# Five kinds of copies dealt out anew and one list of tasks replaced by a longer one, in a fused attention and two-layer feed-forward kernel

## The chip, the cores and the metric

The kernel runs on 1 core of a Trainium2 chip. The metric is device microseconds of one execution. Three runs of the kernel before took 588.29 to 589.33 us, median 588.75 us.

## The reference

Attention of 2 batches, 8 heads, 576 positions and 64 dimensions, with a bias on the scores that a small network makes from the two positions. Its output, 1152 tokens of 512, goes through two feed-forward layers of 512 by 2048 by 512, all in float32:

```python
scores = scale * np.matmul(q, k.transpose(0, 1, 3, 2))
x = (np.log1p(np.abs(rel)) / psi_i)[..., None]     # rel = i - j; psi_i depends on i
bias = np.maximum(x @ w1 + b1, 0.0) @ w2            # 32 hidden, 8 heads
scores = scores + bias.transpose(2, 0, 1)[None]
attn = np.exp(scores - np.max(scores, axis=-1, keepdims=True))
attn = attn / (np.sum(attn, axis=-1, keepdims=True) + 1e-09)
x = np.matmul(attn, v)                              # then to (B*S, H*D)
h = x @ w_in0                                       # first layer
g = s * np.maximum(h, 0.0) ** 2 + b
x = g @ w_out0
h = x @ w_in1                                       # second layer
out = (h * np.tanh(np.log1p(np.exp(h)))) @ w_out1
```

## The kernel before

*Attention.* The work is cut into units: a pair of heads hp, a tile t of 128 queries (the fifth tile has 64), a batch b. The two batches of one (hp, t) make a duo; `ORDER` gives the 20 duos. For a (hp, b) the loads of q and k (`Pair.load`, L486 and L490, SyncE) land in two staging buffers `raw`; a copy packs them into `nat` (`Pair.pack`, L499: for six of the eight pairs, the first two are loaded into `nat` directly); TensorE transposes `nat` to `t` (`Pair.turn`, L527); two copies (`put`, L301 on ScalarE or L303 on VectorE) take `t` out of PSUM into `qk`. For each unit TensorE makes the scores `s` (L571) in PSUM. VectorE adds the bias `nb` and takes the row minimum `mn` of the negated scores (`bias_and_max`, L581), ScalarE the exponential `e` (L591), GpSimd and VectorE the inverse sum and the division (L598, L602, L608). TensorE transposes `e` into `pp` (L622), a copy (`keep`) takes it out as `pt`, and TensorE multiplies with v (`values`, L642). What is left over of a duo's columns goes through `turn_rest` (L663) and `keep_rest`.

*The bias.* It depends on the difference of two positions and on the row, so it is made once, for 36 groups of 16 rows: rectified rows `r` (`bias_row`, L402 on VectorE, L399 on ScalarE), a product on TensorE in two pieces (`bias_products`, L412), copies out as `bo` (`bias_out`, L305 on VectorE, L301 on ScalarE), a mirrored part (`bias_mirror`, L434, on ScalarE or GpSimd), a store to DRAM (`bias_store`, L438). A load `nb` (`load_bias`, L454) reads back the rows of a tile for a pair of heads; it waits for the stores of those rows. The fifth tile, with 64 rows, is the first in `ORDER`.

*The feed-forward layers.* Every float32 product is three products of rounded parts. A weight tile `raw` (512 KB: `rawi` of the first matrix, `rawo` of the second; i0 to i15 and o0 to o15) is loaded (L272, into one of two staging buffers), widened on ScalarE in two steps (L278, L279), joined on VectorE (L284), and split into its rounded part `whi` (`high`, L303) and the difference `wli` (`low`, L297). The tokens stand in three blocks j of 384. A block's hidden group (L1032, 12 matmuls) makes `h` of block j and tile f; relu, a square and two halves follow (L1042, L1045, L1086); the sums (L1109) collect `y`. Hidden groups are named h0_0_4 for layer 0, block 0, tile 4. Eight weight tiles, `WEARLY`, are loaded and converted while the attention still runs; for the others buffers come free when it ends.

*What sets the order.* Nothing is left to a scheduler at run time: each engine works through its own list. `Plan` makes the lists. Every step is a `Task` with an engine, a price in us, what it comes after and the buffers that it takes (`Hold`, numbers in `BUFS`). `WHO` says, a letter for each task, which engine does a copy that two engines could do (v VectorE, a ScalarE, p GpSimd). `SEQ` gives a place in one common row to every task that it names; `Plan.run` takes these in that row, each started as early as its engine and its predecessors allow by the planner's own prices. A task without a place is put in by its start and its rank, once no task of the row that is still due takes the same kind of buffer. Only the order goes into the program; the prices don't.

Of the kernel before, what the change touches and what calls it, by code (L numbers as in the profile page):

```python
# [21 lines left out]
def attention_bias_then_two_moe(ctx: ExitStack, tc: tile.TileContext, ins, out):  # L22
# [24 lines left out]
        'bias_row': 'vvaavavvvvvvvaaaavvvavaavavvvvaavavaavaavavavavvavavavvvvvavvavavavavavvvavvvaavvavvaaavavvvvvvavvaaavaavavavvavvaaaaavvvavvavvaavaavavvvvaaavva',  # L47
        'bias_out': 'avaavvavaaaaavavaaavvaavvaaaaaaavavvavavvaaa',
        'bias_mirror': 'ppapapppppappaaapppppappapppppppapaa',
        'pack': 'vpvpvv',  # L50
        'put': 'vvvaavaaavvvaavavava',
        'keep': 'aaaavvvvaavavvavvvavvaaaavaaaaaavaavavav',
        'keep_rest': 'aaaavvaaaaavavvvvvaa',
# [6 lines left out]
            7, 14, 1, 6, 85, 89, 97, 102, 137, 148, 163, 166, 56, 59, 241, 244,  # L60
        ),
        'bias_row': (
# [5 lines left out]
        ),  # L68
        'bias_products': (
            11, 13, 18, 21, 28, 30, 35, 37, 57, 60, 67, 71, 83, 86, 118, 132, 90, 112, 155, 162, 209, 183, 231, 228, 247, 275, 320, 291, 348, 316,  # L70
            368, 373, 421, 467, 418, 465, 509, 511, 544, 549, 571, 599, 626, 624,
        ),
        'scale_lx': (
            15,
        ),
        'bias_out': (
            16, 17, 24, 26, 33, 34, 39, 43, 62, 63, 77, 84, 87, 98, 133, 139, 114, 125, 164, 174, 217, 195, 245, 233, 260, 295, 343, 298, 357, 333,
            375, 388, 440, 481, 422, 474, 514, 536, 551, 559, 590, 608, 634, 628,
        ),
        'bias_mirror': (  # L80
            47, 29, 36, 45, 69, 116, 120, 182, 145, 160, 177, 180, 222, 200, 258, 254, 271, 344, 351, 353, 389, 400, 446, 454, 472, 493, 489, 479,
            523, 548, 572, 568, 593, 621, 638, 633,
        ),
        'bias_store': (
            54, 40, 38, 48, 82, 121, 124, 191, 149, 169, 181, 192, 253, 249, 293, 261, 296, 346, 360, 356, 427, 403, 452, 458, 475, 503, 494, 499,
            557, 556, 576, 605, 600, 630, 642, 635,
        ),
        'Pair.turn': (
            53, 44, 126, 151, 197, 223, 95, 299,
        ),  # L90
        'Pair.put': (
            61, 58, 68, 80, 50, 134, 140, 158, 161, 159, 207, 211, 232, 230, 229, 100, 99, 306, 308, 309,
        ),
        'Unit.scores': (
            73, 104, 143, 168, 216, 236, 265, 285, 307, 325, 359, 378, 402, 425, 455, 477, 497, 518, 553, 589, 611, 632, 649, 669, 685, 702, 724, 742,
            765, 781, 802, 819, 838, 853, 873, 888, 904, 921, 939, 952,
        ),
        'load_bias': (
# [600 lines left out]
    class Plan:  # L699
# [51 lines left out]
        def run(self):  # L751
# [18 lines left out]
            while given or any(left.values()):  # L770
# [521 lines left out]
```

## Time and profile before

| | |
|---|---|
| median of three runs | 588.75 us |
| the profiled execution | 587.15 us |
| its span | 585.4 us |
| TensorE busy | 570.3 us |
| VectorE busy | 461.5 us |
| ScalarE busy | 374.9 us |
| GpSimd busy | 100.9 us |

The span goes from the first to the last instruction of the program; the profiled execution's own time has a little more around it. A busy time is the sum over an engine's instructions, with nothing of how they stand to each other. The attention fills about the first 180 us, the two feed-forward layers the rest. In the rows below PE is TensorE, PEld its weight load, DVE VectorE, ACT ScalarE, POOL GpSimd, and SP SyncE, from whose queue nearly all DMAs are issued.

### The profile page before, as it was taken

Reading aid. Unit: us, or ns where it says so; the run is one execution under the profiler, and the core shown is the slowest. Engines: PE = TensorE matmul, PEld = TensorE weight load, DVE = VectorE, ACT = ScalarE, POOL = GpSimd, SP = SyncE. Lnnn points to the kernel's source line nnn. Section 1 sums busy time; section 2 is a strip of 40 time slices with the busy share of each in tenths; the row PEclk is TensorE's granted clock in tenths of the full one; section 3 lists DMA queues with packets and bytes.
Section 4 is the critical chain, followed back from the end, with each engine's and each line's share of the span. In section 5 each row is a group of like instructions: output and inputs, shape, how many; then the busy total and the mean of one; then the engine's idle time right before and its main releaser. Section 6 shows DMA issues by size and latency. Waiting matters only on the chain. (4 is left out here: it accounts for less than half of the span.)

```text
span 585.4 us, 12492 instructions
## 1 busy us (share of the span) xinstructions
PE 570.3 (97%) x4740; PEld 509.6 (87%) x4740; DVE 461.5 (79%) x1001; ACT 374.9 (64%) x761; POOL 100.9 (17%) x255
## 2 busy tenths in 40 slices
PE   8699999999999999999999999999999999999997
PEld 5356777888889999999999999989999899999895
DVE  5789899899856999433236999999998788898795
ACT  6799899999965687442224678666554445454453
POOL 2353656567650000000000000000000000000000
PEclk9899999999999999999999999999999999999999
DMA  6899667786404668400000667500000100010001
GB/s 158 239 297 261 209 200 246 238 249 213 146 3 126 234 221 277 151 1 1 1 0 1 209 218 257 180 0 2 0 2 0 55 1 0 1 54 1 1 1 54
DMA packets 50375, 65.99 MB, mean 113 GB/s; under 512 B 17548, under 2 KB 34060, under 8 KB 50316
## 3 DMA queue, kind: packets, MB, share of 16 engines
q1 hardware_dynamic: 50040, 65.11, 35.4%
q8 instruction: 37, 0.61, 0.4%
q14 instruction: 22, 0.18, 0.1%
q10 hardware_dynamic: 276, 0.09, 0.1%
HBM read 51.94 MB, written 13.25 MB: 111 GB/s over the span
## 5 line engine op out<-in xcount | busy, mean ns | idle before, releaser
L608 POOL TENSOR_SCALAR e<-e,rs 128x576 f32<-128x576 f32 (+2 forms) x104 | 66.4, 653 | 17.4 <-DVE rs L602 14.7
L1032 PE MATMUL h<-xh,whi 128*128 128x384 f32 x192 | 64.8, 337 | 0.0
L1032 PE MATMUL h<-yh,wli 128*128 128x384 f32 x192 | 64.7, 337 | 0.0
L1032 PE MATMUL h<-yl,whi 128*128 128x384 f32 x192 | 64.6, 337 | 0.0
L1032 PE MATMUL h<-yh,whi 128*128 128x384 f32 x192 | 64.6, 336 | 0.0
L1032 PE MATMUL h<-xh,wli 128*128 128x384 f32 x192 | 64.4, 335 | 0.0
L1032 PE MATMUL h<-xl,whi 128*128 128x384 f32 x192 | 64.4, 335 | 0.0
L1045 DVE SCALAR_TENSOR_TENSOR u<-h,u 128x384 f32<-128x384 f32 x48 | 26.6, 554 | 42.2 <-ACT u L1042 42.2
L581 DVE CUSTOM_DVE_ANT_0 s<-s,nb 128x576 f32<-128x576 f32 x72 | 52.4, 751 | 6.4 <-PE s L571 5.2
L591 ACT ACTIVATE e<-s,mn 128x576 f32<-128x576 f32 x72 | 55.1, 768 | 3.3 <-DVE mn L581 2.7
L1061 ACT ACTIVATE r<-n,two 128x384 f32<-128x384 f32 x48 | 29.6, 616 | 42.0 <-DVE n L1057 42.0
L571 PE MATMUL s<-qk 64*128 64x144 f32 (+1 forms) x640 | 50.4, 297 | 2.7 <-ACT qk L301 1.5
L571 PEld LDWEIGHTS s<-qk 64*128 64x128 f32 (+1 forms) x640 | 41.7, 178 | 12.0 <-ACT qk L301 3.3
L1042 ACT ACTIVATE u<-h 128x384 f32<-128x384 f32 x48 | 23.2, 483 | 43.5 <-PE h L1032 43.5
L1053 ACT ACTIVATE u<-u 128x384 f32<-128x384 f32 x48 | 25.0, 520 | 33.1 <-DVE u L1050 33.1
L1109 PE MATMUL y<-gl,who 128*128 128x384 f32 (+1 forms) x192 | 44.6, 339 | 0.0
L1109 PE MATMUL y<-gh,wlo 128*128 128x384 f32 (+1 forms) x192 | 44.3, 337 | 0.0
L1109 PE MATMUL y<-gh,who 128*128 128x384 f32 (+1 forms) x192 | 44.3, 337 | 0.0
L1109 PE MATMUL y<-who,gh 128*128 128x512 f32 x144 | 43.3, 395 | 0.8 <-ACT y L1121 0.8
L1109 PE MATMUL y<-wlo,gh 128*128 128x512 f32 x144 | 43.3, 395 | 0.0
L1109 PE MATMUL y<-who,gl 128*128 128x512 f32 x144 | 43.2, 395 | 0.0
L399 ACT ACTIVATE r<-lx,bl 128x368 f32<-128x368 f32 (+17 forms) x63 | 38.6, 651 | 2.2 <-DVE bl L367 2.1
(99 smaller groups left out, 1354.2 us busy)
## 6 DMA issues: line engine op xcount, KB each, us to landing
rawi<-in_moe_w_in_dram SPq DMA_DIRECT2D x32, 512.0 KB, 3.8
rawo<-in_moe_w_out_dram SPq DMA_DIRECT2D x32, 512.0 KB, 4.5
nbias_d<-bo SPq DMA_DIRECT2D x36, 295.5 KB, 2.7
nb<-nbias_d SPq DMA_DIRECT2D x32, 288.0 KB, 4.5
natv<-in_v_dram SPq DMA_DIRECT2D x16, 128.0 KB, 5.5
out_dram<-ob SPq DMA_DIRECT2D x8, 256.0 KB, 2.5
raw<-in_q_dram SPq DMA_DIRECT2D x6, 288.0 KB, 5.9
raw<-in_k_dram SPq DMA_DIRECT2D x6, 288.0 KB, 4.9
```

The lines of the kernel that those rows point to most:

```text
L399: nc.scalar.activation(out=r, in_=src, func=AF.Relu, bias=bl[:, g : g + 1])
L571: nc.tensor.matmul(self.ps[rows, x if self.both else 2 * j + x, o : o + PIECE], st.qk[d, 0, self.q0 : self.q0 + self.w], st.qk[d, 1, c0 : ...
L581: nc.vector.tensor_tensor_reduce(out=self.s[n][:m], in0=self.ps[:m, 2 * n : 2 * n + 2, :HALF], in1=nb[:m].rearrange("p (n j) -> p n j", n= ...
L591: nc.scalar.activation(out=self.e[:m, (S + REST) * n :][:, :S], in_=self.s[n][:m].rearrange("p n j -> p (n j)"), func=AF.Exp, bias=self.mn ...
L608: nc.gpsimd.tensor_scalar(self.e[:m, y : y + w], self.e[:m, x : x + w], self.rs[:m, n : n + 1], 0.0, op0=ALU.mult, op1=ALU.add)
L1032: nc.tensor.matmul(self.ph, w[:, c * P : (c + 1) * P], x[:, c, :], start=(c == 0 and n == 0), stop=(c == KD - 1 and n == 2),)
L1042: nc.scalar.activation(out=self.u, in_=self.ph, func=AF.Relu)
L1045: nc.vector.scalar_tensor_tensor(self.u, self.ph, 0.0, self.u, op0=ALU.max, op1=ALU.mult)
L1053: nc.scalar.activation(out=self.z, in_=self.z, func=AF.Exp)
L1061: nc.scalar.activation(out=self.r, in_=self.n, func=AF.Ln, bias=two)
L1109: nc.tensor.matmul(o, a, c, start=(f == 0 and i == 0), stop=(f == NF - 1 and i == 2))
```

## The change

The instructions are the same; their order and, for the copies, their engines are others. Three things change. `WHO` deals the copies out anew: among others the first six `pack` copies go from `vpvpvv` to `avvapp` (in the planner's count, not in the order of time), and the four mirrors first in the count go to ScalarE. `SEQ` is another row: it had 1010 places, which ended with the first 16 hidden groups and held 8 weight tiles; it now has 1298, and holds 20 weight loads of the first matrices, 12 of the second (`load`), 32 conversions, and the blocks of the first layer up to sums of the second block. Last, the planner's prices of transfers (`us` the issue, `mb` the size) are changed, and its rule for tasks that have no place in the row: such a task now waits until no task of the row is left for its *engine*, where before it looked at kinds of buffers.

```diff
...
-        'bias_mirror': 'ppapapppppappaaapppppappapppppppapaa',
-        'pack': 'vpvpvv',
...
+        'bias_mirror': 'aaaapapappppppppaapapappppaapppaapap',
+        'pack': 'avvapp',
...
     SEQ = {
...
         'Pair.load': (
-            7, 14, 1, 6, 85, 89, 97, 102, 137, 148, 163, 166, 56, 59, 241, 244,
+            3, 8, 2, 14, 58, 74, 101, 103, 120, 123, 154, 165, 1, 57, 253, 262,
...
@@ -757,11 +791,11 @@
             pipe, port, form = PIPE, 0.0, 0
             self.made = []
 
-            due = [h.what for t in given for h in t.takes]
+            due = [t.engine for t in given]
 
             def key(t):
                 at = self.ready(t)
-                if at is None or t.seq is None and any(h.what in due for h in t.takes):
+                if at is None or t.seq is None and t.engine in due:
                     return None
                 dry = DRY if t.engine == "PE" and t.form != form else 0.0
                 start = max(at, free[t.engine], port if t.port else 0.0)
@@ -793,8 +827,7 @@
                     left[t.engine].remove(t)
                 else:
                     given.pop()
-                    for h in t.takes:
-                        due.remove(h.what)
+                    due.remove(t.engine)
                 for h in t.takes:
                     self.holds[h.what].append(h)
                 self.made.append(t)
@@ -824,7 +857,7 @@
 
     firstnb = [add("none", 0.0, 3, lambda: None)]
     stores, rowed = {}, []
-    lx0 = add("SP", 0.45, -150, load_lx, mb=0.3)
+    lx0 = add("SP", 0.45, -150, load_lx, mb=0.27)
     lx0 = add("POOL", 0.8, -150, scale_lx, after=[lx0])
 
     def clear_all():
@@ -858,7 +891,7 @@
             h1.users.append(o)
             outs.append(o)
         m = add_any({"a": ("ACT", 0.0008 * (BW - w) + 0.1), "p": ("POOL", 0.0012 * (BW - w) + 0.15)}, at + GRANK + 2, bias_mirror, G, after=outs)
-        stores[G] = add("SP", 0.5, at - 50, bias_store, G, after=[m], mb=0.3)
+        stores[G] = add("SP", 0.42, at - 50, bias_store, G, after=[m], mb=0.22)
         hb.users.append(stores[G])
 
 
@@ -870,7 +903,7 @@
         hr, hn, hold, hl = Hold("raw"), Hold("nat"), Hold(big), Hold("one")
         cut = n < CUT
         loads = [
-            fetch(1.35 if cut else 0.65, key, LLEAD, 0.6 if cut else 0.3, st.load, nm, cut, takes=[hn if cut else hr] if nm == "q" else [])
+            fetch(1.35 if cut else 0.65, key, LLEAD, 0.42 if cut else 0.28, st.load, nm, cut, takes=[hn if cut else hr] if nm == "q" else [])
             for nm in "qk"
         ]
         loads[1].behind = loads[:1]
@@ -898,7 +931,7 @@
                 h = Hold("nb")
                 after = [stores[G] for G in range(u.q0 // (RI * RI), (u.q0 + u.w) // (RI * RI))]
                 nbh[u.hp, u.t, n] = h, add("SP", 1.2 if u.both else 0.58, at - (80 if i > 1 else 400), load_bias, u.hp, u.t, u.heads(n), after=after,
-                                           takes=[h], mb=0.29)
+                                           takes=[h], mb=0.27)
                 nbh[u.hp, u.t, n][1].soft = [*issued[-1:], *([scored[i - NLEAD]] if i >= NLEAD else [])]
                 issued.append(nbh[u.hp, u.t, n][1])
                 firstnb[0].past = issued[:1]
@@ -919,7 +952,7 @@
             exps.append(x)
             if n == 0 and firsts[u.hp, u.b] == i:
                 hl = Hold("lastv")
-                lv = add("SP", 1.9, 10 * i + VRANK, stacks[u.hp, u.b].load_v, takes=[hl], mb=0.4)
+                lv = add("SP", 1.85, 10 * i + VRANK, stacks[u.hp, u.b].load_v, takes=[hl], mb=0.37)
                 lv.soft = [load, s]
                 valued[u.hp, u.b] = add("POOL", 0.55, 10 * i, stacks[u.hp, u.b].spread_v, after=[lv, zeros])
                 hl.users.append(valued[u.hp, u.b])
@@ -1002,7 +1035,7 @@
             load = w.load
         hr, hf, hw = Hold("wraw" + two), Hold("wf" + two), Hold(f"w{'a' if f < EARLY else 'b'}{nm}")
         new = [] if early else [opened]
-        t = add("SP", 0.42, at - 20, load, after=[ended, *(new if two else [])], takes=[hr], mb=0.52)
+        t = add("SP", 0.42, at - 20, load, after=[ended, *(new if two else [])], takes=[hr], mb=0.45)
         t = add("ACT", 1.12, at, w.widen, after=[t], takes=[hf])
         t = add("DVE", 0.6, at + 1, w.join, after=[t])
         hr.users.append(t)
```

Three places in the lists, a row an instruction: the line, the operation, what it writes and reads. The last number of a name counts buffers; what stands ahead of it tells the tile: of a unit batch, pair of heads, tile of queries (s_1_0_4: batch 1, heads 0, tile 4), of a pair batch and heads (t_0_3, t_3 for short), of a bias product its group and first column (bias_4_0), of a weight layer and tile (rawi_0_3 is i3 of layer 0). The lines of the changed kernel are 34 higher.

TensorE, in the first 30 us, where the pair `t_0_3` is transposed ahead of the second unit's scores `s_1_0_4`, before:

```order
L412 MATMUL bias_2_272_415<-r_11_349,w2b_123 32x272
L412 MATMUL bias_4_0_425<-r_16_365,w2b_123 32x512
L412 MATMUL bias_4_0_425<-r_17_358,w2b_123 32x512
L412 MATMUL bias_4_0_425<-r_18_376,w2b_123 32x512
L412 MATMUL bias_4_0_425<-r_19_385,w2b_123 32x512
L527 MATMUL t_0_3_441<-ident_66,nat_0_3_422 128x64 x18
L571 MATMUL s_1_0_4_473<-qk_1_0_273 64x144 x8
```

and now:

```order
L446 MATMUL bias_2_272_417<-r_11_381,w2b_123 32x272
L561 MATMUL t_0_3_433<-ident_66,nat_0_3_431 128x64 x18
L446 MATMUL bias_4_0_461<-r_16_425,w2b_123 32x512
L446 MATMUL bias_4_0_461<-r_17_400,w2b_123 32x512
L446 MATMUL bias_4_0_461<-r_18_427,w2b_123 32x512
L446 MATMUL bias_4_0_461<-r_19_405,w2b_123 32x512
L605 MATMUL s_1_0_4_479<-qk_1_0_302 64x144 x8
```

The four products of bias group 4 stood ahead of `t_0_3` and now stand behind it, ahead of the scores.

VectorE at the same place (`nat_0_3` is the packed pair, `mn_0_0_4_0` the minimum of the first unit), before:

```order
L402 TENSOR_SCALAR r_10_381<-lx0_113,bl_124 128x544
L402 TENSOR_SCALAR r_8_387<-lx0_113,bl_124 128x544
L303 COPY nat_0_3_422<-raw_0_3_327 128x1152
L581 ISA s_0_0_4_0_436,mn_0_0_4_0_437<-s_0_0_4_367,nb_0_4_0_378 128x576
L581 ISA mn_0_0_4_0_437 128x1
L305 TENSOR_SCALAR bo_2_420<-bias_2_272_415,li_115 128x272
L303 COPY qk_0_3_442<-t_0_3_441 128x576
```

and now:

```order
L436 TENSOR_SCALAR r_10_403<-lx0_113,bl_124 128x544
L436 TENSOR_SCALAR r_19_405<-lx0_113,bl_124 128x512
L337 COPY qk_1_0_302<-t_1_0_301 128x64x8
L615 ISA s_0_0_4_0_422,mn_0_0_4_0_423<-s_0_0_4_385,nb_0_4_0_371 128x576
L615 ISA mn_0_0_4_0_423 128x1
L339 TENSOR_SCALAR bo_2_453<-bias_2_0_411,li_115 128x272
L436 TENSOR_SCALAR r_23_455<-lx0_113,bl_124 128x496
L339 TENSOR_SCALAR bo_2_453<-bias_2_272_417,li_115 128x272
L337 COPY qk_0_3_434<-t_0_3_433 128x576
```

The copy `nat_0_3` is gone from VectorE ahead of the minimum (it is on GpSimd now); in its place stands a copy `qk_1_0`, and copies of bias sums have moved up.

SyncE's queue near the end of the attention (the rows nb are loads of bias rows: heads, tile, first head), before:

```order
L272 DMA rawi_0_3_2612<-in_moe_w_in_dram 128x4x256
L454 DMA nb_3_2_1_2634<-nbias_d_76 128x1x576
L272 DMA rawo_0_2_2736<-in_moe_w_out_dram 128x1024
L454 DMA nb_0_3_1_2744<-nbias_d_76 128x1x576
L272 DMA rawi_0_4_2768<-in_moe_w_in_dram 128x4x256
L454 DMA nb_0_3_0_2781<-nbias_d_76 128x1x576
L272 DMA rawi_0_5_2856<-in_moe_w_in_dram 128x4x256
L454 DMA nb_2_1_0_2874<-nbias_d_76 128x1x576
L454 DMA nb_1_0_0_2978<-nbias_d_76 128x1x576
L454 DMA nb_1_0_1_2982<-nbias_d_76 128x1x576
L454 DMA nb_2_1_1_2999<-nbias_d_76 128x1x576
L272 DMA rawi_0_6_3064<-in_moe_w_in_dram 128x4x256
```

and now:

```order
L306 DMA rawi_0_1_2966<-in_moe_w_in_dram 128x4x256
L996 DMA s_sb_71<-in_moe_s_dram 128x1
L997 DMA b_sb_72<-in_moe_b_dram 128x1
L488 DMA nb_1_0_1_2970<-nbias_d_76 128x1x576
L488 DMA nb_2_1_0_3052<-nbias_d_76 128x1x576
L488 DMA nb_2_1_1_3221<-nbias_d_76 128x1x576
L306 DMA rawo_0_1_3322<-in_moe_w_out_dram 128x1024
L306 DMA rawi_0_3_3413<-in_moe_w_in_dram 128x4x256
L306 DMA rawo_0_2_3438<-in_moe_w_out_dram 128x1024
L306 DMA rawi_0_4_3458<-in_moe_w_in_dram 128x4x256
L306 DMA rawo_0_4_3505<-in_moe_w_out_dram 128x1024
L306 DMA rawi_0_5_3543<-in_moe_w_in_dram 128x4x256
```

Before, weight loads stood between the loads of bias rows; now those shown after rawi_0_1 come behind the last one.

## Rows read from the trace of the kernel before

**Rows 1.** The profile page, its first line.

```profile
span 585.4 us, 12492 instructions
```

**Rows 2.** Busy time of each engine by stretch: start:end, length, busy us, granted clock.

```profile
120.00:140.00 20.00, 19.04 (x309) 16.11 (x307) 19.79 (x51) 19.77 (x42) 14.43 (x24) 1.00 0.70 222
...
180.00:380.00 200.00, 200.00 (x1161) 199.77 (x1158) 140.01 (x275) 114.84 (x218) 3.66 (x32) 1.00 0.41 134
...
380.00:400.00 20.00, 19.16 (x102) 17.72 (x102) 17.39 (x37) 12.45 (x24) 0.00 (x0) 1.00 0.00 0
```

**Rows 3.** Who TensorE waited for: us in total, times, longest.

```profile
PE t L527 <- DVE mn L581: 2.0, 1, 2.0
...
PE s L571 <- ACT qk L301: 1.5, 1, 1.5
...
PE bias L412 <- ACT bo L301: 1.0, 3, 0.6
```

**Rows 4.** Timeline of TensorE, 19 to 34 us: start, us, instruction.

```profile
19.42 2.38 PE L412 MATMUL bias<-r,w2b 128*32 128x272 f32 x24 [0.44 <-DVE r L402]
...
23.80 0.77 PE L527 MATMUL t<-ident,nat 64*128 64x64 f32 x18 [1.99 <-DVE mn L581]
...
26.10 2.18 PE L571 MATMUL s<-qk 64*64 64x144 f32 x16 [1.54 <-ACT qk L301]
...
32.89 1.20 PE L571 MATMUL s<-qk 64*64 64x144 f32 x16
```

**Rows 5.** Busy time by stretch, 26 to 30 us; the 0.52 and 0.63 are the clock.

```profile
26.00:28.00 2.00, 1.90 (x16) 1.66 (x16) 1.03 (x2) 2.00 (x5) 1.46 (x5) 0.52 1.11 261
...
28.00:30.00 2.00, 2.00 (x20) 0.52 (x16) 1.67 (x3) 1.33 (x4) 0.19 (x1) 0.63 1.07 216
```

**Rows 6.** Timeline of VectorE and ScalarE, 21 to 26 us.

```profile
21.71 1.35 DVE L303 COPY nat<-raw 128x1152 f32<-128x1152 f32 x1 [2.44 <-DMA raw<-in_k_dram]
...
22.98 0.75 DVE L581 CUSTOM_DVE_ANT_0 s<-s,nb 128x576 f32<-128x576 f32 x1
...
25.40 0.65 ACT L301 ACTIVATE qk<-t 128x576 f32<-128x576 f32 x1 [0.76 <-DVE qk L303]
```

**Rows 7.** The DMA queue's issues at 19 us, and issues by line.

```profile
19.08 1.18 SPq L454 DMA_DIRECT2D nb<-nbias_d  x2
...
nb<-nbias_d SPq DMA_DIRECT2D x8, 144.0 KB, 3.2
```

**Rows 8.** Who TensorE waited for, 100 to 175 us.

```profile
PE s L571 <- DVE mn L581: 0.7, 2, 0.5
...
PE pp L622 <- POOL e L608: 0.5, 1, 0.5
```

**Rows 9.** Weight conversions, 100 to 172 us: count, ns min/median/max.

```profile
L278 ACT ACTIVATE wfi<-rawi x6: 677/688/697, 113.7 to 152.7; 128x512 int32<-128x512 uint16 x6
...
L284 DVE SCALAR_TENSOR_TENSOR wfi<-rawi,wfi x6: 672/689/1127, 116.3 to 154.4; 128x512 int32<-128x512 int32 x6
...
L284 DVE SCALAR_TENSOR_TENSOR wfo<-rawo,wfo x4: 686/690/727, 119.1 to 142.2; 128x512 int32<-128x512 int32 x4
```

**Rows 10.** Timeline, 173 to 190 us, and landing of the first weights' loads.

```profile
173.42 0.44 PE L1032 MATMUL h<-xh,whi 128*128 128x384 f32 x1
...
173.53 1.03 ACT L301 ACTIVATE pt<-pp 128x1024 f32<-128x1024 f32 x1 [0.25 <-PE pp L622]
...
175.91 0.71 PE L622 MATMUL pp<-ident,e 64*128 64x64 f32 x16
...
182.08 0.42 DVE L303 CAST whi<-wfi 128x512 fp32r<-128x512 f32 x1
...
182.41 0.55 DVE L1045 SCALAR_TENSOR_TENSOR u<-h,u 128x384 f32<-128x384 f32 x1
...
182.88 0.68 DVE L297 TENSOR_TENSOR wli<-wfi,whi 128x512 fp32r<-128x512 f32 x1
...
189.02 0.34 PE L1032 MATMUL h<-xh,whi 128*128 128x384 f32 x1
...
DMA to landing us min/median/max: 3.5/3.8/4.6
```

More of the change, by code (lines that the diff above doesn't have):

```diff
@@ new lines, in attention_bias_then_two_moe @@
+            369, 385, 420, 462, 429, 465, 536, 511, 538, 568, 592, 610, 659, 612,
+        ),
+        'bias_out': (
+            12, 13, 23, 25, 32, 35, 44, 46, 64, 66, 76, 77, 94, 96, 140, 141, 114, 119, 167, 188, 217, 202, 249, 234, 257, 278, 333, 297, 376, 329,
+            377, 418, 425, 466, 430, 481, 548, 530, 539, 583, 603, 611, 668, 627,
+        ),
+        'bias_mirror': (
+            26, 37, 40, 47, 67, 81, 151, 149, 130, 183, 174, 189, 223, 222, 310, 241, 299, 316, 352, 355, 391, 362, 411, 489, 442, 483, 504, 505, 624,
+            531, 556, 602, 634, 651, 669, 662,
+        ),
@@ L90, in attention_bias_then_two_moe @@
         ),
         'Pair.put': (
-            61, 58, 68, 80, 50, 134, 140, 158, 161, 159, 207, 211, 232, 230, 229, 100, 99, 306, 308, 309,
+            73, 50, 62, 86, 59, 138, 134, 157, 158, 156, 199, 207, 226, 227, 225, 100, 99, 314, 318, 313,
+        ),
+        'clear_all': (
+            63,
+        ),
+        'load_bias': (
+            69, 102, 164, 236, 255, 273, 267, 327, 397, 396, 413, 405, 404, 477, 527, 526, 552, 550, 562, 551, 688, 664, 713, 702, 712, 755, 715, 722,
+            771, 804, 809, 805, 849, 855, 880, 923,
@@ L133, in attention_bias_then_two_moe @@
         ),
         'Pair.spread_v': (
[L135 to L143 removed]
+            153, 152, 216, 263, 288, 321, 452, 456,
@@ L160, in attention_bias_then_two_moe @@
         ),
         'Weights.load': (
-            655, 660, 692, 709, 749, 729, 770, 804,
+            720, 721, 770, 950, 853, 848, 977, 982, 990, 1010, 1037, 1053, 1063, 1069, 1078, 1110, 1125, 1132, 1151, 1168,
+        ),
+        'Weights.widen': (
+            752, 802, 832, 975, 960, 935, 987, 998, 1011, 1047, 1033, 1058, 1038, 1066, 1055, 1105, 1064, 1117, 1083, 1124, 1102, 1146, 1114, 1158,
+            1144, 1184, 1153, 1202, 1167, 1219, 1189, 1227,
+        ),
+        'Weights.join': (
+            763, 825, 841, 981, 966, 948, 988, 1001, 1012, 1048, 1034, 1073, 1039, 1076, 1061, 1107, 1077, 1118, 1091, 1138, 1103, 1147, 1120, 1172,
+            1145, 1185, 1166, 1203, 1169, 1222, 1198, 1228,
+        ),
@@ L167, in attention_bias_then_two_moe @@
[L167 to L177 removed]
+            854,
         ),
         'Block.hidden': (
[L180 removed]
+            972, 973, 978, 983, 984, 1003, 1006, 1007, 1004, 1005, 1013, 1019, 1008, 1017, 1018, 1028, 1043, 1052, 1075, 1090, 1104, 1119, 1135, 1157,
@@ new lines, in attention_bias_then_two_moe @@
+            1170, 1191, 1208, 1215, 1226, 1241, 1258, 1263, 1279, 1287,
+        ),
+        'load': (
+            996, 1042, 1065, 1074, 1093, 1123, 1131, 1150, 1152, 1174, 1210, 1211,
+        ),
+        'Block.relu': (
+            997, 1014, 1020, 1035, 1049, 1081, 1087, 1115, 1122, 1142, 1159, 1173, 1190, 1192, 1209, 1232, 1236, 1242, 1259, 1264, 1283, 1288,
+        ),
+        'Block.square': (
+            999, 1016, 1023, 1036, 1051, 1082, 1089, 1116, 1126, 1143, 1163, 1181, 1193, 1216, 1214, 1233, 1237, 1245, 1260, 1266, 1284, 1290,
+        ),
@@ new lines, in attention_bias_then_two_moe @@
+        'Block.high': (
+            1000, 1021, 1024, 1054, 1057, 1086, 1101, 1121, 1136, 1154, 1171, 1187, 1194, 1217, 1220, 1238, 1239, 1246, 1271, 1272, 1285, 1291,
+        ),
+        'Block.low': (
+            1009, 1026, 1044, 1070, 1071, 1098, 1106, 1129, 1137, 1160, 1175, 1188, 1199, 1218, 1221, 1240, 1257, 1247, 1280, 1278, 1286, 1292,
+        ),
+        'Block.sums': (
+            1031, 1027, 1030, 1029, 1032, 1045, 1046, 1067, 1068, 1079, 1080, 1096, 1097, 1112, 1113, 1133, 1134, 1148, 1149, 1164, 1165, 1177, 1178,
+            1195, 1197, 1212, 1213, 1223, 1224, 1230, 1231, 1243, 1250, 1248, 1261, 1244, 1270, 1267, 1269, 1268, 1273, 1274, 1275, 1281, 1282, 1293,
+            1294, 1295, 1296, 1297,
+        ),
@@ L181, in attention_bias_then_two_moe @@
+        'scaled_sum': (
+            1251, 1249, 1262, 1255,
+        ),
+        'high_sum': (
+            1254, 1252, 1265, 1276,
+        ),
+        'low_sum': (
+            1256, 1253, 1289, 1277,
         ),
```

109 lines of the change are left out of this document (42 added, 67 removed), and 28 rows, old and new, of the table SEQ.

## The prediction

> **What bounds the kernel now.** I read the page's first line, then busy time by stretch, then who TensorE waited for, then the timeline around its longest waits. The span is 585.4 us [rows 1]; the profiled execution took 587.15, 1.75 around the span, and is itself 1.6 under the median of the runs, 588.75. From 180 to 380 us TensorE is busy for 200.00 of 200.00 us, and about the layer border at 380 to 400 for 19.16 of 20 [rows 2]. The matmuls of the two feed-forward layers are the same before and after, so no order can shorten that part except by those 0.84 us. What can move lies in the attention part, the first 180 us, where TensorE still waits. The largest waits there are 2.0 us of the transpose t for the row minimum mn, 1.5 us of the scores s for the copy qk, and 1.0 us in three pieces for bias sums bo [rows 3]. The first two lie side by side. The timeline shows it: a bias product ends at 19.42 + 2.38 = 21.80, t stands from 23.80 to 24.57, and s begins at 26.10 [rows 4]: in 4.3 us TensorE works for 0.77. And the wait has a tail. In the 2 us from 26 the granted clock is 0.52, in the next 2 us 0.63 [rows 5], which is the 1.2 GHz level for about 3.4 us (0.48/0.5 of the first two microseconds and 0.37/0.5 of the next: 1.92 + 1.48). The score group there takes 2.18 us, and the same group at 32.89, at full clock, 1.20 [rows 4]. Work done at half speed for 3.4 us has cost 1.7 us.
>
> So this one place costs 2.0 + 1.5 + 1.7 = 5.2 us. Everything else that TensorE waits for in the attention part is small: 0.7 and 0.5 us late in it [rows 8], where VectorE (19.79) and ScalarE (19.77 of 20) are full from 120 to 140 and TensorE is not (19.04) [rows 2].
>
> **The change, part by part.** No instruction's work is changed; copies move between engines and the order moves on all five. The new transfer sizes in the planner alter no transfer, only the planner's own plan.
>
> *The place at 20 to 28 us.* The chain there is: minimum (needs scores and the loaded bias nb), transpose t_3 into the same PSUM banks, the two qk copies out of them, next scores. The minimum begins at 22.98, just as the copy nat (21.71, 1.35 long) ends; that copy itself stood on VectorE for 2.44 us, waiting for a load of k [rows 6]. In the new order this copy is on GpSimd, so the minimum no longer waits behind it. Then nb is late next: its two issues begin at 19.08 and end at 20.26, and such a load lands 3.2 us after issue [rows 7], between 22.9 and 23.5 if the median holds; the minimum began at 22.98, so it was at the earlier edge of that. In the new order the stores that nb waits for stand in the order 32, 33, 34, 35 with all mirrors of them on ScalarE, and a load of q has gone ahead of the first loads; that may bring nb some tenths forward. The minimum gains between 0 (nb as late as before) and 1.3 (the start of the copy that is gone, 22.98 - 21.71). I take 0.4, near the lower end, because the load is the nearest row.
>
> The product bias_4 moves from ahead of t_3 to behind it. It does not shorten the chain: the next scores need the qk copies, which end at 25.40 + 0.65 = 26.05 [rows 6], and those hang on the minimum. But it changes what TensorE does in the gap: from t on it now has 0.77 + about 1.2 us of work before the scores, with some 0.5 us of idle time, where before it had 0.77 and then 1.54 of idle time. The unbroken wait ahead of t becomes about 1 us longer, since bias_4 no longer fills its start. So the question is whether the clock falls again. The rows show one fall only, and shorter waits (the three for bias sums, the longest 0.6) [rows 3] without one. I take it that the clock stays up, as the work right ahead of the scores is more than doubled: gain 1.7. The bounds are 0 (it falls just the same) and 1.7; a longer stretch at half speed would cost up to another 1.7.
>
> By the Trainium skill, "TensorE: Matmul & The Clock Gate", Part 1, the gate lowers the clock after TensorE has been idle and only sustained work raises it again, whichever instruction it waited for. By that rule the longer wait ahead of t speaks against the change: the clock would fall earlier, bias_4 would run at half speed, and the 1.7 would not come back; that is the first rival below. The trace here agrees that a wait lowers the clock (one fall, after the longest wait); no run here yet shows which wait is long enough.
>
> *40 to 175 us.* In the order before, ten weight tiles are widened on ScalarE and joined on VectorE between 113 and 155 us [rows 9]: each two widening steps of 0.69 and one join of 0.69, and eight of them also a rounding copy and a difference of 0.42 and 0.68 [rows 10]. In the new order three stand before the last minimum and seven behind it. That takes 7 x 1.38 = 9.7 us from ScalarE and, with the rounding of the five that had it, 7 x 0.69 + 5 x 1.10 = 10.3 us from VectorE, out of the stretch where both are full. Against it ScalarE gets eight more pt copies (31 for 23 in the order), at most 8 x 1.03 [rows 10] = 8.2 us, which VectorE loses. What TensorE waited for there is 0.7 + 0.5 = 1.2 us [rows 8]; ScalarE is hardly freer than before, so not all of it goes: I take 0.8, bounds +1.2 (the waits double) and -1.2.
>
> *The head of the first layer.* The seven weights are cheap at their new place only if they come in time. They are the price that the list pays; I cost it at nothing because VectorE and ScalarE have room there, but the cover is thin (second rival).
>
> *The layer border and the second layer.* TensorE's order there differs only by a hidden group or two that changes place. The 0.84 us stay; bounds are 0 and twice that.
>
> Sum: -0.4 - 1.7 - 0.8 = -2.9 us. On the profiled execution 587.15 - 2.9 = 584.25; on the median 588.75 - 2.9 = 585.85, and I give 585.8.
>
> **The rivals.** *The clock falls all the same.* Then only 0.4 + 0.8 = 1.2 is left: 587.5. For it: the wait ahead of t gets longer. Against it: twice the work follows at once.
>
> *The weights come late: slower.* Place: the hidden group of the fifth block, h0_0_4, which begins at 189.02 before [rows 10]; its weight i4 was then joined since 155. Now i4's load stands behind that of i3, and a staging pair of two buffers lets it go only when i3 is joined. i3's widening stands on ScalarE behind the last pt copy, whose transpose pp ends at 175.91 + 0.71 = 176.6: copy until 177.6, widening 1.38, join 0.69: 179.7. Load of i4 3.8 us at the median, 4.6 at the longest [rows 10]: 183.5 to 184.3. Widening, join and, between them on VectorE, a difference of another weight, two squares and i4's own copy and difference: 1.38 + 0.69 + 0.68 + 2 x 0.55 + 0.42 + 0.68 = 4.95: 188.4 to 189.2 against 189.02, or about 188.6 if the list reaches the group a little sooner. So it holds by half a microsecond or fails by as much, and the next weights follow the same chain at the same distance. From that point each load that lands at 4.6 and not 3.8 pushes TensorE by 0.8; three in a row make 2.4, and a wait of this length may drop the clock for another 1.7. With 0.4 to 1.2 of the gain kept that is 588.75 + 2.4 - 0.6 = 590.5, up to 592.
>
> The Trainium skill, "DMA: Bandwidth & Descriptors", gives a fixed 2.0 us and bytes over 436 GB/s for a load; by it 512 KB would take 3.2, an estimate, and the chain would hold by 1.2. The traced 3.8 is longer, and the chain above goes by that.
>
> *Nothing comes of it.* The plan's gain is on paper only: other waits of the same size open elsewhere in a list that is new everywhere. 588.75.
>
> **How the numbers follow.** Chances: forecast 0.45; the clock falls 0.22; nothing 0.12; late weights 0.21. A difference under 0.2%, 1.2 us, can't be told from none. Faster by more: nearly all of the forecast (0.44), half of the second case (0.11), a little of the third (0.02): 0.57. Slower by more: 0.21 of the late weights and 0.03 of the third: 0.24. The rest is 0.19. The likeliest case alone spans 584.0 (the minimum gains 1.3, all small waits go) to 587.2. The range for 8 in 10 runs from 583 (the place at 20 us gives back most of its 5.2) to 590.5.
>
> **What would show it.** Right: no second clock level between 20 and 32 us; the wait for mn under 3 us and none of 1.5 for qk behind it; the copy nat gone from VectorE ahead of the first minimum; the first hidden group some 3 us before 173.4; TensorE busy for 20 of 20 us from 180 on. Wrong: clock 0.5 again near 24 to 30 us; waits of h or y for weights or their loads at 183 to 200 us; new waits on ScalarE between 60 and 160. The forecast falls if the part before the first hidden group is no shorter.

## The result, and the profile after

Slower: 592.49 us median of 20 runs (589.53 to 598.22) against 588.68 for the kernel before (585.95 to 592.42); the ratio of the means is 1.0075, 95% interval 1.005 to 1.010. The forecast was 585.8, the range 583 to 590.5. The profiled execution of the changed kernel took 595.22, 2.7 over its median, with a span of 593.4; that of before [rows 1] was 1.6 under its own. So the two profiled executions stand 8.1 us apart where the medians stand 3.8 apart, and a wait that one profile shows need not stand in every execution.

The page's first line, and the view of what TensorE waited for (us in total, times, longest), beside which [rows 3] stand:

```profile
span 593.4 us, 12514 instructions
```

```profile
PE t L561 <- DVE mn L615: 3.3, 1, 3.3
PE s L605 <- DVE mn L615: 2.9, 1, 2.9
PE y L1142 <- ACT y L1154: 2.3, 2, 1.4
PE s L605 <- DVE rs L636: 1.6, 1, 1.6
...
PE y L1142 <- ACT gh L1119: 1.0, 1, 1.0
```

The wait of t for the row minimum is 3.3 us where it was 2.0, the one of s for the copy qk behind it is gone, and there are four that were small or absent before.

*20 to 30 us.* Busy time by stretch of the changed kernel (start and end, length, busy us of TensorE, its weight loads, VectorE, ScalarE and GpSimd, then the granted clock and the DMA share):

```profile
22.00:24.00 2.00, 0.00 (x0) 0.00 (x0) 0.87 (x3) 0.07 (x1) 0.00 (x0) 0.78 1.05 282
24.00:26.00 2.00, 1.96 (x22) 1.27 (x26) 1.80 (x5) 0.80 (x2) 0.19 (x1) 0.50 0.79 207
...
28.00:30.00 2.00, 2.00 (x20) 0.98 (x16) 0.71 (x3) 1.00 (x2) 0.65 (x2) 0.52 0.76 160
```

TensorE is idle for the whole of 22 to 24, and the clock falls in that wait; it is at 0.50 (the 1.2 GHz level) up to 29.9 us, where before it was low for 3.4 us from 26 on [rows 5].

*VectorE and the bias loads.* The view of what VectorE waited for in the first 175 us, first of the kernel before, then of the changed one:

```profile
DVE s L581 <- DMA nb<-nbias_d: 0.9, 1, 0.9
```

```profile
DVE s L615 <- DMA nb<-nbias_d: 9.4, 4, 3.3
```

0.9 us have become 9.4. The minimum (L615) needs the rows nb of the bias, and four times they are not there. The timeline of the changed kernel, with the SyncE issues that lie ahead of the second and the last two waits:

```profile
23.13 0.76 DVE L615 CUSTOM_DVE_ANT_0 s<-s,nb 128x576 f32<-128x576 f32 x1 [2.55 <-DMA nb<-nbias_d]
...
46.40 0.56 SPq L488 DMA_DIRECT2D nb<-nbias_d  x1
47.01 0.58 SPq L472 DMA_DIRECT2D nbias_d<-bo  x1
47.64 0.64 SPq L524 DMA_DIRECT2D raw<-in_q_dram  x1
48.31 0.61 SPq L472 DMA_DIRECT2D nbias_d<-bo  x1
48.97 0.55 SPq L488 DMA_DIRECT2D nb<-nbias_d  x1
...
54.40 0.76 DVE L615 CUSTOM_DVE_ANT_0 s<-s,nb 128x576 f32<-128x576 f32 x1 [1.68 <-DMA nb<-nbias_d]
...
117.47 0.80 SPq L472 DMA_DIRECT2D nbias_d<-bo  x2
122.79 2.46 SPq L488 DMA_DIRECT2D nb<-nbias_d  x4
...
126.03 0.76 DVE L615 CUSTOM_DVE_ANT_0 s<-s,nb 128x576 f32<-128x576 f32 x1 [1.87 <-DMA nb<-nbias_d]
...
130.13 0.76 DVE L615 CUSTOM_DVE_ANT_0 s<-s,nb 128x576 f32<-128x576 f32 x1 [3.26 <-DMA nb<-nbias_d]
```

Two places are to be seen. Around 47 us the two halves of the same bias rows (nb_0_0_0 and nb_0_0_1) stand apart, with two stores and a load of q between them. And the last two stores of bias rows leave at 117.47; the loads that need them stand behind them and leave at 122.79. In the kernel before the two halves are issued together, and the last stores go 11 us earlier:

```profile
45.16 1.96 SPq L454 DMA_DIRECT2D nb<-nbias_d  x2
...
106.57 1.20 SPq L438 DMA_DIRECT2D nbias_d<-bo  x2
```

What SyncE's queue waited for from 112 to 132 us in the changed kernel says that those loads were held by the stores:

```profile
SPq L488 <- DMA nbias_d<-bo: 4.3, 2, 2.4
```

*The layers.* Busy time by stretch, first before, then after (start and end, length, then TensorE's busy time):

```profile
180.00:240.00 60.00, 60.00 (x358) 59.83 (x355) 53.87 (x106) 44.40 (x85) 3.66 (x32) 1.00 0.69 226
380.00:420.00 40.00, 39.16 (x202) 35.89 (x202) 37.18 (x78) 24.43 (x47) 0.00 (x0) 1.00 0.00 1
```

```profile
180.00:240.00 60.00, 58.52 (x367) 57.11 (x368) 52.47 (x102) 42.71 (x79) 3.21 (x29) 1.00 0.69 219
380.00:420.00 40.00, 37.74 (x199) 35.00 (x198) 37.18 (x77) 25.92 (x50) 0.00 (x0) 1.00 0.09 33
```

TensorE's idle time is 0.00 and 0.84 us before, 1.48 and 2.26 after. The first of the two begins here (ScalarE, SyncE and TensorE in the changed kernel):

```profile
184.25 0.38 SPq L306 DMA_DIRECT2D rawi<-in_moe_w_in_dram  x1
...
189.57 0.67 ACT L312 ACTIVATE wfi<-rawi 128x512 int32<-128x512 uint16 x1 [2.35 <-DMA rawi<-in_moe_w_in_dram]
...
193.28 0.94 PE L1142 MATMUL y<-gh,who 128*128 128x386 f32 x4 [1.03 <-ACT gh L1119]
```

The weight tile i4 is issued at 184.25 and widened at 189.57, after 2.35 us in which ScalarE waited for it; the relu stands behind it there, and sums wait 1.03 us for their gh. The hidden group h0_0_4 comes right behind these sums. The first hidden group of all, which began at 173.42 before [rows 10] and was forecast some 3 us earlier, begins later:

```profile
178.16 0.42 PE L1065 MATMUL h<-xh,whi 128*128 128x384 f32 x1
```

From there to the end of the span it is 415.2 us, before 412.0. So in these two profiles both parts have become longer.

### The profile page after: what moved, and what is told of

Read it like the earlier page. It is cut to its first block, busy times and chain, and to the rows that moved or that the text cites. A ratio compares the mean times of both kernels' runs of the same rounds, so it can differ in the third digit from the quotient of the medians.

```text
span 593.4 us, 12514 instructions
## 1 busy us (share of the span) xinstructions
PE 571.6 (96%) x4740; PEld 509.6 (86%) x4740; DVE 460.4 (78%) x1002; ACT 378.5 (64%) x764; POOL 98.7 (17%) x251
## 5 line engine op out<-in xcount | busy, mean ns | idle before, releaser
L615 DVE CUSTOM_DVE_ANT_0 s<-s,nb 128x576 f32<-128x576 f32 x72 | 52.6, 752 | 22.2 <-PE s L605 12.5
L642 POOL TENSOR_SCALAR e<-e,rs 128x576 f32<-128x576 f32 (+2 forms) x104 | 64.2, 632 | 28.8 <-DVE rs L636 22.5
L676 PE MATMUL po<-pt,natv 128*64 128x128 f32 (+1 forms) x640 | 40.6, 271 | 0.0
```

Source lines behind the costliest of these rows:

```text
L615: nc.vector.tensor_tensor_reduce(out=self.s[n][:m], in0=self.ps[:m, 2 * n : 2 * n + 2, :HALF], in1=nb[:m].rearrange("p (n j) -> p n j", n= ...
L642: nc.gpsimd.tensor_scalar(self.e[:m, y : y + w], self.e[:m, x : x + w], self.rs[:m, n : n + 1], 0.0, op0=ALU.mult, op1=ALU.add)
L676: nc.tensor.matmul(po[D * j : D * j + D], va[:, c, j, :], p, start=(c == 0), stop=(c == NQ - 1))
```

## The experiments

Theory 1: the loss lies where minimums wait for rows nb that the new list loads later. Theory 2: it lies in the feed-forward layers, in weights that come late. Theory 3: at 20 us, loads that were put ahead hold up the first nb. All ratios are to the kernel before, with their 95% intervals; "idle" is TensorE's.

**The list cut in two.** The attention part of one list with the layers' part of the other. The edit of the first, in the changed kernel (copies dealt as before, `HEAD` is the row before):

```diff
+    for what, places in SEQ.items():
+        old = HEAD.get(what, ())
+        SEQ[what] = old + tuple(1000 + s for s in places[len(old):])
```

> The attention part of the row before, copies dealt as before, and behind it the changed row's places for the weights from the ninth on, the blocks and the sums. Theory 1: as before, 588 to 589.5. Theory 2: 588.7 + 1.0 + 1.0 + 1.5 = 592.2, with waits at 190 to 235 us and at the layer border.

Measured: 0.9997 (0.9982 to 1.0013). VectorE waits 0.0 us for nb. Its profile shows TensorE idle for some of what theory 2 named:

```profile
180.00:240.00 60.00, 59.38 (x363) 58.32 (x362) 49.51 (x96) 39.90 (x76) 3.65 (x31) 1.00 0.65 208
380.00:420.00 40.00, 38.57 (x201) 35.47 (x200) 37.18 (x77) 24.89 (x48) 0.00 (x0) 1.00 0.01 3
```

that is 0.62 and 1.43 us, yet the time can't be told from that of before. The second half of the pair keeps the changed attention part and drops the rest:

```diff
+    for what in ("load", "Block.relu", "Block.square", "Block.high", "Block.low", "Block.sums", "scaled_sum", "high_sum", "low_sum"):
+        del SEQ[what]
+    SEQ["Block.hidden"] = SEQ["Block.hidden"][:16]
+    for what in ("load", "widen", "join", "high", "low"):
+        SEQ["Weights." + what] = SEQ["Weights." + what][:8]
...
-            due = [t.engine for t in given]
+            due = [h.what for t in given for h in t.takes]
```

> The attention part of the changed row, with its eight early weights and first 16 hidden groups; all places of later weights, blocks and sums are dropped and the planner's old rule for unplaced tasks is back, so the layers are ordered as before. Theory 1 (the loss is in the attention): 592 to 593, the same wait at 124 to 131. Theory 2 (the loss is in the weights and the layers): 589 to 590, no wait at 190 to 235 and 0.8 at the layer border.

Measured: 1.0101 (1.0074 to 1.0127), and VectorE waits 10.7 us for nb in its profile (an execution 6.4 us over the median, so of this one only the kind of wait is used). The loss comes with the new attention part, which here takes in the eight early weight tiles, and the new places for the later weights and the layers cost nothing that can be measured: theory 2 falls in the form it had. What the new attention part does to the layers is still open here.

**The last bias rows.** Group 22 made earlier, and the stores of 20 and 22 behind their mirrors:

```diff
# bias_row, bias_products, bias_out, bias_mirror, bias_store
-  595, 635, 648, 641, 631, 597,
+  595, 612.3, 612.5, 612.4, 612.2, 597,
...
-  592, 610, 659, 612,
+  592, 610, 625.5, 612,
...
-  603, 611, 668, 627,
+  603, 611, 628.5, 627,
...
-            531, 556, 602, 634, 651, 669, 662,
+            531, 556, 602, 634, 651, 639.5, 662,
...
-            625, 564, 563, 614, 696, 652, 695, 663,
+            625, 564, 563, 614, 641.5, 652, 641.4, 663,
```

> The changed kernel (592.5) with the bias group 22 of the last tile made some 45 places earlier in the row, and the stores of groups 20 and 22 put right behind their mirrors. Theory 1, the loads nb of the last tile stand behind stores that leave at 117.5 us, and VectorE waits 1.87 + 3.26 us for them at 124 to 130: the wait of 2.9 us of TensorE and the 1.1 us of half clock behind it go, 588.5 to 589.5, stores away by about 112 us. Theory 2, the loss lies in the feed-forward layers' weights (1.0 us at 192, 1.0 at 220 to 235, 1.5 more at the layer border): the wait moves elsewhere, 592 to 593.

Measured: 1.0062 (1.0043 to 1.0082). The stores and the loads behind them:

```profile
104.49 11.38 SPq L472 DMA_DIRECT2D nbias_d<-bo  x6
115.93 4.33 SPq L488 DMA_DIRECT2D nb<-nbias_d  x6
```

The waits at 124 to 130 are gone (VectorE waits 4.0 us for nb in all, none of it after 80 us), but the time falls by 0.13% only, within the intervals. The wait is real and the price that I took from one profile too high: in other profiles of the same list at that place VectorE waits 4.7 (raw_late), 1.8 (nb_early) and 0.5 us (nb_first).

**One load moved, both ways.** nb_0_0_1 right behind nb_0_0_0 in the changed kernel, and the opposite in the kernel before:

```diff
-            69, 102, 164, 236, 255, 273, 267, 327,
+            69, 102, 164, 236, 236.5, 273, 267, 327,
```

> The changed kernel with one load moved on SyncE: nb_0_0_1 goes from behind two stores and a load of q to right behind nb_0_0_0. Theory 1, the loss lies where VectorE waits for loads nb that were issued later than before (1.7 us at 53): that wait goes, VectorE waits some 2 us less for nb, and the ratio to before falls from 1.0075 to 1.004 to 1.005 (591 to 592 against 589). Rival, the wait only moves to the loads that are now behind it (q, and the stores for the next tile): ratio unchanged, 1.0065 to 1.0085.

```diff
-            75, 128, 154, 234, 238, 262, 268, 300,
+            75, 128, 154, 234, 253.5, 262, 268, 300,
```

> The kernel before with the same load moved the other way: nb_0_0_1 behind the loads of q and k and the two stores that follow it. Theory 1: the wait of VectorE for nb appears at 50 to 56 us, 1.5 to 3 us long, TensorE waits 1.5 to 2.5 us there, ratio 1.002 to 1.005. Rival, the wait is hidden by other work in the order of before: ratio 0.998 to 1.001.

Measured: 1.0044 (1.0025 to 1.0063) for the first, 1.0052 (1.0032 to 1.0072) for the second. The first interval still overlaps that of the changed kernel (1.005 to 1.010), so by itself it is not clear of noise; the second is clear of 1. It is one instruction, on an engine that computes nothing. In the kernel before with the load moved back, the wait stands where theory 1 put it:

```profile
46.12 0.55 SPq L454 DMA_DIRECT2D nb<-nbias_d  x1
...
49.33 0.57 SPq L454 DMA_DIRECT2D nb<-nbias_d  x1
...
54.90 0.76 DVE L581 CUSTOM_DVE_ANT_0 s<-s,nb 128x576 f32<-128x576 f32 x1 [2.18 <-DMA nb<-nbias_d]
```

2.18 us on VectorE, where neither profile of the kernel before has one. Behind it the clock falls as well, to 0.66 from 56 to 58 us and to 0.50 in the next two:

```profile
58.00:60.00 2.00, 2.00 (x24) 0.86 (x16) 2.00 (x8) 0.84 (x3) 0.00 (x0) 0.50 0.88 287
```

Both together, as edited above:

> The edits of bias_early and nb_early together. Theory 1: VectorE waits for nb only at 20 to 24 us (1.3 to 2.6), and with both waits gone the time is that of before, or within 0.3% of it: ratio 0.999 to 1.003. Rival, what the copies dealt anew and the order of the rest cost is not in these waits: ratio 1.004 to 1.006.

Measured: 1.0031 (1.0017 to 1.0045), clearly under 1.005, the lower end of the changed kernel. By the middle values, 0.44 of 0.75%, more than half of the loss is these two places; neither theory's band was met (0.999 to 1.003 and 1.004 to 1.006). What is left in its profile:

```profile
DVE s L615 <- DMA nb<-nbias_d: 3.2, 2, 2.9
```

```profile
115.00:180.00 65.00, 64.10 (x1043) 56.16 (x1042) 47.38 (x130) 57.09 (x121) 37.10 (x80) 1.00 0.45 144
180.00:240.00 60.00, 57.47 (x326) 56.75 (x325) 51.28 (x100) 40.55 (x76) 3.30 (x25) 1.00 0.68 221
380.00:420.00 40.00, 38.31 (x199) 35.05 (x198) 37.19 (x77) 24.98 (x49) 0.00 (x0) 1.00 0.01 3
```

nb is waited for at 20 us still (2.88 of the 3.2). TensorE is idle for 0.90 us at 115 to 180, less than the 1.63 of before: here the freer VectorE that the forecast counted on does give something. At 180 to 240 it is 2.53 for 0.00, at the border 1.69 for 0.84.

**The place at 20 us.** One load of q put back behind the first stores, and in another kernel two loads put behind nb:

```diff
-            3, 8, 2, 14, 58, 74, 101, 103, 120, 123, 154, 165, 1, 57, 253, 262,
+            3, 8, 2, 14, 58, 74, 101, 103, 120, 123, 154, 165, 56.5, 57, 253, 262,
```

> The changed kernel with one load moved on SyncE: the q rows of the pair 0_3, which now stand ahead of the first loads nat (issue 0.7 us), go to where they stood before, behind the first stores. Theory 3, these rows delay the first loads and through them the load nb that the first minimum waits for (2.55 us on VectorE): nb lands 0.7 us or more earlier and the minimum begins at 22.4 or earlier, 591.0 to 591.8. Rival, nb waits for the stores and those for the bias rows, which need none of these loads: the minimum stays at 23.1, 592 to 593.

```diff
-            3, 8, 2, 14, 58, 74, 101, 103, 120, 123, 154, 165, 1, 57, 253, 262,
+            3, 8, 2, 14, 69.6, 74, 101, 103, 120, 123, 154, 165, 1, 69.5, 253, 262,
```

> The changed kernel with two loads moved on SyncE: k of the pair 0_3 and q of the pair 0_1 go from just ahead of the first load nb to behind it. Theory 3a, these 576 KB share the DMA with nb (14.3 to 23 us) and make it land late: nb lands under 4.5 us after its issue, the minimum begins at 22.3 or earlier, TensorE's wait for mn is under 2.6, ratio 1.0055 to 1.007. Rival, nb is held by its stores alone: the minimum stays at 22.8 to 23.4, and t may now wait for the late copy nat; ratio 1.0065 to 1.009.

Measured: 1.0086 (1.0053 to 1.0119) and 1.0075 (1.0043 to 1.0107). With q back the minimum begins at 23.37: theory 3 falls in the form it had. (The place that q went back to is right ahead of nb, so this run put three loads there and not two.) With the two loads behind nb it begins at 21.43, 1.7 earlier:

```profile
17.83 1.20 SPq L488 DMA_DIRECT2D nb<-nbias_d  x2
...
21.43 0.76 DVE L615 CUSTOM_DVE_ANT_0 s<-s,nb 128x576 f32<-128x576 f32 x1 [0.92 <-DMA nb<-nbias_d]
...
23.12 1.15 POOL L533 TENSOR_SCALAR nat<-raw 128x1152 f32<-128x1152 f32 x1 [5.74 <-DMA raw<-in_k_dram]
...
24.33 0.90 PE L561 MATMUL t<-ident,nat 64*128 64x64 f32 x18 [3.65 <-POOL nat L533]
```

So the traffic ahead of nb seems to delay it, as 3a says: in the ten other profiles in which the first minimum waits for nb, all with two or three loads right ahead of it, it begins between 22.01 (bias_early) and 23.53 (both_early). It is one profile against ten that spread by 1.5 us. And k came late in its place: the copy nat on GpSimd waits for it, and t begins at 24.33, for 24.04 in the changed kernel. What the one load gives the other takes, and the time is that of the changed kernel.

**The early weights.** both_early with the conversions of the eight early tiles at the places of before, the same with the copies pt and prt dealt as before, one with five tiles some 5 us earlier than in the changed list, and the kernel before with its tiles at the changed places:

```diff
+    for what, places in {
+        "Weights.load": (655, 660, 692, 709, 749, 729, 770, 804),
+        "Weights.widen": (679, 689, 715, 736, 789, 758, 796, 831),
...
+    }.items():
+        SEQ[what] = tuple(p + 50.5 for p in places) + SEQ[what][8:]
```

> both_early with the first eight weight tiles loaded and converted where the row before has them (its places plus 50.5), so seven are ready before the last minimum and not three; TensorE's order is the same. Theory 1a, what is left of the loss (0.3%) is TensorE's idle time of 1.5 to 2.5 us at 180 to 240 us, where the tiles come late: it goes to 0.5 or less, ratio 0.998 to 1.001. Rival, the 9.7 and 10.3 us of conversions only move back into 115 to 175 us, where ScalarE has more copies than before: idle time there grows by 1 us or more, ratio 1.002 to 1.005.

```diff
-        'keep': 'aavaaaavavaavvavaavavaaaaaaaaaaaaaaavaaa',
+        'keep': 'aaaavvvvaavavvavvvavvvaaaavaaaaaavaavavav',
```

> weights_early with the copies pt and prt dealt as before (keep and keep_rest: 23 pt copies on ScalarE, not 31). If weights_early lost its 1.1% because eight more copies of 1.03 us and the conversions don't fit into ScalarE together at 115 to 180 us, TensorE's idle time there falls from 8.65 us to under 4 and the ratio from 1.0137 to 1.002 to 1.006. Rival, the conversions stand at wrong places in this row whoever makes the copies: idle 7 us or more, ratio 1.010 or more.

```diff
+        "Weights.load": (720, 721, 770, 892.5, 853, 848, 909.5, 927.5),
+        "Weights.widen": (752, 802, 832, 921.5, 903.5, 886.5, 940.5, 958.5),
+        "Weights.join": (763, 825, 841, 925.5, 907.5, 890.5, 944.5, 962.5),
...
```

> both_early with the conversions of the last five of the eight early tiles some 5 us earlier than there (o3 at place 886 for 935, o2 at 958 for 998), between both_early and weights_early. If the late tiles cost what TensorE idles at 180 to 240 us, and ScalarE and VectorE have room from 160 us on, the idle time there goes under 1 us and the ratio from 1.0031 to 0.999 to 1.002. Rival, the conversions cost as much where they go: idle at 150 to 180 us grows by 1 us or more, ratio 1.002 to 1.006.

In the last of the four the places of the changed row stand in the row of before, plus 0.5.

> The kernel before with the first eight weight tiles loaded and converted at the places of the changed row. Theory 1a: TensorE idles 1 to 2.5 us at 180 to 240 us, where it idled 0.0; ratio 1.001 to 1.004. Rival, the weights are hidden (head_old_tail_new moved only the later ones and cost nothing): ratio 0.998 to 1.001.

Measured: 1.0137 (1.0109 to 1.0164), 1.0300 (1.0275 to 1.0325), 1.0102 (1.0084 to 1.0121) and 1.0079 (1.0052 to 1.0107). In weights_early the idle time goes where the rival said:

```profile
115.00:180.00 65.00, 56.35 (x928) 48.58 (x926) 47.51 (x130) 54.73 (x118) 36.88 (x71) 1.00 0.46 152
180.00:240.00 60.00, 60.00 (x408) 58.69 (x405) 45.76 (x89) 40.67 (x77) 5.59 (x32) 1.00 0.60 194
```

0.00 us at 180 to 240, and 8.65 at 115 to 180. Dealing the copies as before makes it worse still (8.79 us there, and 5.12 at 40 to 80), so the eight copies on ScalarE are not what fills the stretch: that explanation falls. In weights_mid 4.45 us are idle at 115 to 180. What VectorE waited for at 150 to 185:

```profile
DVE wfo L327 <- ACT rawo L322: 2.8, 2, 2.1
```

This is weights_mid. A join in VectorE's list waits for its widening, which stands behind exponentials and a copy pt in ScalarE's, and the minimum stands behind the join. Both steps had been moved earlier in the row, and still their places in the two lists do not fit. (The profile of weights_mid also has a wait of 3.01 us for nb at 60 us, where that of both_early has none.) The fourth kernel shows the other side: late tiles cost the list of before 0.79%, more than the 0.1 to 0.4% expected; in its profile TensorE is idle for 2.89 us at 115 to 180, 0.46 at 180 to 240 and 2.53 at the border, so not where theory 1a had put it.

**The kernel before once more.**

> The kernel before, profiled once more, for how much the places differ from one execution to the next. If its first profile (1.5 us under the median) was a lucky one, waits of 0.5 to 2.5 us stand at 200 to 235 us and at the layer border, as in the profile of head_old_tail_new; if the changed places of the layers make those waits, none stands there but the 0.8 at the border.

Measured: 589.13. Busy time by stretch:

```profile
115.00:180.00 65.00, 61.69 (x999) 54.31 (x999) 52.62 (x138) 54.98 (x120) 39.00 (x72) 1.00 0.45 146
180.00:240.00 60.00, 60.00 (x369) 59.58 (x368) 52.54 (x104) 43.55 (x82) 3.86 (x31) 1.00 0.69 225
380.00:420.00 40.00, 39.58 (x207) 36.52 (x206) 37.14 (x77) 24.45 (x47) 0.00 (x0) 1.00 0.00 1
```

No wait at 180 to 240, 0.42 at the border; 3.31 at 115 to 180 where the first profile has 1.63. The 0.00 at 180 to 240 stands in before_nb_late too, so the waits there belong to the changed lists. The wait at the border does not: before_nb_late has the order of before on TensorE, VectorE and ScalarE and idles for 2.18 us there. And the attention part differs by some 2 us from one execution to the next.

The profiles settle one thing more. Each of these lines is the start of the first hidden group, in before_again, both_early, weights_early and before_weights_late:

```profile
175.82 0.44 PE L1032 MATMUL h<-xh,whi 128*128 128x384 f32 x1
```

```profile
173.00 0.42 PE L1065 MATMUL h<-xh,whi 128*128 128x384 f32 x1
```

```profile
182.23 0.42 PE L1074 MATMUL h<-xh,whi 128*128 128x384 f32 x1
```

```profile
175.85 0.45 PE L1041 MATMUL h<-xh,whi 128*128 128x384 f32 x1
```

From there to the end of their spans (587.3, 588.5, 594.9 and 591.8 us) it is 411.5, 415.5, 412.7 and 416.0 us. This stretch takes 411.5 to 413.5 us in all seven profiles in which the eight early tiles are loaded and converted at the places of before or, in weights_mid, between the two, and 414.6 to 416.0 in seven with the changed places (419.6 in the eighth, the one 6.4 us over its median). both_early and weights_early have the same order on TensorE, so the 2.8 us between them come with the places of the tiles. The late tiles cost some 3 us behind the first hidden group, the border included. In both_early that is more than the whole loss that is left: its first hidden group begins no later than in either profile of the kernel before.

## Why the prediction was wrong

*What bounds.* Right: from 240 to 380 us TensorE is busy throughout in the profile of after too, and the time is made in the attention part and in what it hands on.

*The minimum, -0.4.* The mechanism was right, the size at the lower bound: the copy nat left VectorE, and nb was late next, as late as before (23.13 for 22.98). The tenths that the reordered stores were to bring were there at the issue (17.94 for 19.08) and gone at the landing: 5.2 us where 3.9 were enough before. I took the median of eight loads, 3.2 [rows 7], for a load that has a load of q and one of k, 576 KB, right ahead of it in both orders. Without them it takes 3.6 (nb_first); why it lands no earlier when it is issued earlier was not isolated.

*The clock, -1.7.* Wrong; the first rival had it. TensorE idles 3.29 us ahead of t, the clock falls in that wait, and t, bias_4 and the scores all ran at half speed. That twice the work stands behind the wait came too late to matter. The 1.7 did not come back; that more was lost is not shown. Over the first 40 us the mean granted clock is 0.96 in both profiles of the kernel before and 0.91 in that of the changed one, but it is also 0.91 in two kernels with the order of before at that place (head_old_tail_new, before_weights_late) and 0.96 in eight with the changed attention part. The rule that the prediction had weighed against itself (the Trainium skill, "TensorE: Matmul & The Clock Gate", Part 1: idle time lowers the clock, sustained work raises it) said so; the trace agrees, with 0.78 in the two idle microseconds and 0.50 behind them.

*40 to 175 us, -0.8 with bounds of 1.2 either way: the first of the two steps that failed.* I judged the stretch by how full ScalarE and VectorE are and by what TensorE had waited for, and costed what left them. What the new list changed there was the path of the bias rows: product, copy, mirror, store, load, minimum. Before, VectorE waited 0.9 us for it in all, so the rows of the waits did not point there, and I followed SyncE's list only at the end of the attention. The order of the changed kernel had both places in plain sight: a store and a load between two loads of one unit, and tile 2's last stores directly ahead of its first loads. Moving those two back takes the ratio from 1.0075 to 1.0031, some 2.6 us, and moving one load the other way in the kernel before costs it 0.52%. With both moved back the first hidden group begins no later than before, in one profile, so a gain of the kind that I forecast may exist beside this path; its size is not shown.

*The head of the first layer, 0: the second step that failed.* I put the price of the late tiles at nothing; they cost some 3 us behind the first hidden group (414.6 to 416.0 us for 411.5 to 413.5), and in the kernel before the ratio with them alone moved is 1.0079. The second rival had the tile and the place: i4, at h0_0_4. Its chain began later than I had it (i3 was widened at 182.23 and not at 177.6) and the load took 5.3 us, over the 4.6 that I took for the longest; the wait came through ScalarE's list, where the relu stands behind the widening, and not through h itself. 1.48 us of idle time stand between 180 and 240 us, against the rival's 2.4; that the border would wait longer too the rival did not say.

*The layer border, 0 with bounds of 0 and 1.7.* Inside the bounds in size: 2.26 for 0.84 in the profile, and 1.2 to 3.1 in every kernel but the one before. What makes it was not isolated: it is 2.18 in before_nb_late, where only a load at 46 us was moved.

The first two rivals together were what happened, and the bias rows are what the third had said in general, that other waits open elsewhere; I had given each a chance of its own as though only one could be true. The last 0.3% stands by the profiles behind the first hidden group, where both_early loses 3.5 to 4.0 us, some 3 of them by the late tiles; ahead of that group it is no later than before. What stays open is how to take that away: no kernel here did it without a larger loss elsewhere. No version beat the kernel before.

## What to carry to other kernels

Of a new order, follow first the longest chain that no row of waits shows, because in the old order it was early: here store, load and minimum, over three queues. Compare where its first and last links stand in each engine's list, and what has come between two loads of one consumer. A wait that the list opens costs twice where the clock falls behind it, as it did at 20 to 30 us in all profiles but one and behind the wait at 54 us in before_nb_late (not behind that of 1.68 us at 54 us in the changed kernel). A step moved forward on one engine stops that engine if what it needs is not done by then on another. And a step that is moved back is not free because engines have room at its new place: cost the whole chain from there, and split the measured time at the border of the parts to see in which of them it is lost.

## What the runs showed of the hardware

The same 288 KB (two halves of 144) were there 3.6 us after their first issue with no load right ahead (nb_first, one profile). With two or three loads of 288 KB ahead it was 3.5 to 5.6 us in ten profiles, 5.2 in the changed kernel; the shortest times are of those kernels in which it was issued last (19.2 us and later). The clock fell in every profile with the waits at 20 to 30 us but one: in weights_early_keep it is 1.00 over the first 40 us, although TensorE idles for 9.0 of them; why was not tried. And the spread of the runs grew with the order: 589.5 to 598.2 for the changed kernel, 586.0 to 592.4 for the one before, from the same instructions.
